# Leaving out GpSimd's normalisation of the attention weights: V as the streamed operand, with a column of ones

## The chip, the cores and the metric

The kernel runs on one core of a Trainium2 chip. The metric is the time of one execution on the device, in microseconds, as the median of several runs. The engines of a core work through queues of their own: TensorE (PE, with its weight loads as PEld), VectorE (DVE), ScalarE (ACT), GpSimd (POOL), and the sync engine (SP), which here issues nearly all transfers.

## The reference, cut to what matters

Three layers follow each other. Everything is float32.

1. Attention over 4 batches, 8 heads, 576 positions, 64 columns a head, causal with a window of 128 and a linear position bias:

```
scores = where(mask, q @ k.T / sqrt(64) + bias, -1e9);  e = exp(scores - max(scores))
attn_out = (e / (sum(e) + 1e-9)) @ v
```

2. A soft mixture of 8 experts with 4 slots each over the 2304 x 512 result `x`: `logits = x @ phi`; softmax over the tokens of a slot gives the slot inputs `d.T @ x`; each expert computes `relu(s @ w1[e]) @ w2[e]` (w1 and w2 together are 33.5 MB); softmax over the slots of a token combines the slot outputs.

3. A feed-forward layer: `h = x @ w_in; out = max(0.01 h, h) @ w_out`.

## The kernel before, in words

**Attention by pairs.** Two heads make a pair; 16 pairs (index i) run through a software pipeline. In `XO` each step of a pair has a place in units of one head; step `S` of pair i stands at 2 i + XO[S]. In `YO` the steps of a batch (8 heads) stand likewise. The program sorts all steps by place and emits them in this order, so that each engine's queue is in this order too, and several pairs are under way at once.

The steps of a pair: q and k are loaded, copied by GpSimd into another order of columns (`RK`, `RQ`, line L254), transposed by TensorE (`TK`, `TQ`, `TR`) and evacuated (`EK`, `EQ`, `ER`). `SX` and `SY` compute the scores in tiles of 64 x 192. VectorE adds the mask, writes the negated result and keeps the maximum (`M..`, L313). ScalarE takes the exponential and the row sum as accumulator (`E..`, L324). VectorE adds 1e-9 and inverts the sums (`UX`, `UY`, L330 and L331). GpSimd multiplies the weights by the inverses (`N..`, L338): nine instructions a pair. TensorE transposes the weights, 13 a pair (`F..`, L349), ScalarE and VectorE evacuate them (`C..`, L355).

`AV` (`attend`, L381) multiplies: V is the loaded operand and the transposed weights are streamed, 64 columns at a time, in 34 products. The result comes out with the head's columns on the partitions, as `xT`, which the logits need; it is evacuated by two ScalarE copies (L389) and a VectorE copy (L394), and a GpSimd copy (L397) pads the last 64 positions. `TX` transposes it back in five transposes (L404, L405), and VectorE copies the result into `xs` (`XS`, L409 and L410), which the slot inputs need.

**Scores' and outputs' buffers** in PSUM come from a ring of eight banks (`gt`), used in program order.

**Transfers.** Loads of q, k, v and the two shifts of v inside SBUF stand in the list `bulk`, with the place from which each may go; expert weights stand in the list `low`, in pieces of 128 x 512 (256 KB). `issue(n)` is called three times in each head unit, at the places of `XI`. It sends what is due of `bulk`; a call that sent nothing of it adds a credit (L0/3 pieces, after unit 26 L1/3) and sends as many pieces of `low` as the credit allows. A last call sends all that is left. 71 pieces have places that are free from the start (14 slots of four, and 15 others); six more go where q and k lay, and 20 where attention's other buffers lay, after the last pair's steps. The other 31 go into the slots p0 to p7 when the products with w1 have used them.

**The end of attention.** `TAIL` is the order of steps after the last `AV`. Then L776 multiplies the slot inputs by w1 (16 units of eight instructions) and L828 the hidden values by w2 (16 units). The first weights of the feed-forward layer, and then its products (L952), follow.

Of the kernel before, what the change touches and what calls it, by code (L numbers as in the profile page):

```python
# [18 lines left out]
def attn_softmoe_ffn(ctx: ExitStack, tc: tile.TileContext, q, k, v, phi, w1, w2, w_in, w_out, cst_in, out):  # L19
# [24 lines left out]
    YO = {"lg": 3.759, "lga": 4.885, "lh": 7.61, "lgc": 7.945, "lx": 8.496, "pm": 8.866, "ln": 9.053, "lnc": 9.191,  # L44
          "bm": 9.764, "tm2": 10.535, "tm3": 10.743, "bmv": 10.891, "dxv": 11.042, "bmx": 11.191, "tme": 11.431,
          "dxa": 11.452, "bt": 11.466, "btv": 12.289, "sl": 12.592, "bta": 12.637, "cb": 12.647, "slv": 12.811,
          "ds": 13.568, "cb2": 13.895, "cb3": 14.066, "dsv": 14.57, "cb4": 14.676}
    LAST = {"li": 6.795, "lgi": 6.853}
    ZA = {"DQK": 0.8, "DV": 0.3, "DVS": 0.3, "DVO": 1.4, "W0": -2.2, "EARLY": 0.8, "L0": 2.55, "L1": 3.6, "I1": 0.7769, "I2": 0.7995, "I3": 0.86}
# [1036 lines left out]
```

## Time and profile before

| | |
|---|---|
| median of 3 runs | 469.11 us (467.61 to 469.34) |
| profiled execution | 469.3 us, span 467.6 us, mean granted TensorE clock 0.967 of full |
| TensorE busy (loads) | 424.2 us, 91% (320.1 us, 68%) |
| VectorE, ScalarE, GpSimd busy | 245.7 us, 234.6 us, 144.2 us |
| transfers | 73.85 MB, 158 GB/s over the span |

The span runs from the first to the last instruction of the profiled execution; its own time is 1.7 us longer. A line number names the line of the kernel that issued an instruction. The granted clock is given as a share of 2.4 GHz.

### The profile page before, as it was taken

The page shows a single profiled execution, that of the slowest core. Times are in us where ns is not written, and L with a number is a line of the kernel's source. Part 1 is how long each engine was busy: PE and PEld are TensorE (multiplying, and loading weights), DVE is VectorE, ACT ScalarE, POOL GpSimd, SP SyncE. Part 2 cuts the span into 40 slices and gives each one's busy share as a digit, 9 for nine tenths or more (in the row PEclk, how much of TensorE's full clock was granted, in tenths as well). Part 3 has the DMA queues.
Part 4 walks back from the last instruction along what each step waited for, and adds up shares of the span by engine and source line. Part 5 has one row for each costly group of instructions (what it writes and reads, how often), then busy time and mean ns, then how long its engine had stood idle before and what let it go on. Part 6 is the DMA issues. An engine that isn't in the chain of part 4 may idle for free.

```text
span 467.6 us, 10684 instructions
## 1 busy us (share of the span) xinstructions
PE 424.2 (91%) x4012; PEld 320.1 (68%) x4012; DVE 245.7 (53%) x786; ACT 234.6 (50%) x706; POOL 144.2 (31%) x231
## 2 busy tenths in 40 slices
...
GB/s 156 149 219 208 148 227 171 178 187 173 177 178 193 117 239 379 382 382 386 392 405 391 208 78 2 179 1 0 1 1 1 1 0 137 0 0 136 0 69 68
DMA packets 63140, 73.85 MB, mean 158 GB/s; under 512 B 27760, under 2 KB 37360, under 8 KB 63088
## 3 DMA queue, kind: packets, MB, share of 16 engines
...
## 4 chain that ended last, share of the span: by engine, by line
PE 56%; POOL 5%; DMA 3%; SPq 2%; DVE 1%; issue 1%; ACT 0%; DVEq 0%; POOLq 0%
PE acc L952 42%; POOL ss L338 5%; PE ph L929 4%; PE pb L776 4%; DMA p<-in_moe_w_dram 3%; SPq L793 2%; PE ph L879 1%; DVE ss L313 1%; PE g L296 1%; PE ph L888 0%; PE pb L828 0%; PE g L622 0%; PE g L349 0%; PE g L381 0%; PE g L552 0%
## 5 line engine op out<-in xcount | busy, mean ns | idle before, releaser
L952 PE MATMUL acc<-p,p 128*128 128x512 f32 x648 | 158.9, 390 | 0.0
L952 PEld LDWEIGHTS acc<-p,p 128*128 128x128 f32 x648 | 120.7, 188 | 24.7 <-issue 1.7
L338 POOL TENSOR_SCALAR ss<-ss,sm 128x192 f32<-128x192 f32 (+1 forms) x144 | 102.3, 730 | 8.2 <-ACT ss L324 5.2
L942 DVE TENSOR_TENSOR p<-ar,p 128x384 fp32r<-128x384 f32 x96 | 53.1, 556 | 91.8 <-ACT ar L938 91.7
L934 ACT ACTIVATE p<-ph 128x384 fp32r<-128x384 f32 (+1 forms) x97 | 47.5, 491 | 92.7 <-PE ph L929 92.6
L349 PE MATMUL g<-ident,ss 128*128 128x128 f32 x208 | 45.3, 301 | 28.6 <-POOL ss L338 26.5
L324 ACT ACTIVATE ss<-ss,mx 128x192 f32<-128x192 f32 x144 | 61.8, 434 | 3.1 <-DVE mx L313 3.1
L349 PEld LDWEIGHTS g<-ident,ss 128*128 128x128 f32 x208 | 23.5, 142 | 45.9 <-POOL ss L338 44.6
L952 PE MATMUL acc<-b,p 128*128 128x512 f32 x216 | 53.9, 394 | 0.0
L722 POOL TENSOR_TENSOR p<-ar,p 128x512 fp32r<-128x512 f32 x8 | 10.6, 1324 | 136.0 <-ACT p L722 119.5
L938 ACT ACTIVATE ar<-ph 128x384 f32<-128x384 f32 x96 | 47.0, 490 | 0.0
L313 DVE CUSTOM_DVE_ANT_0 ss<-g,ar 128x192 f32<-128x192 f32 x128 | 38.6, 354 | 15.3 <-PE g L296 15.2
L952 PEld LDWEIGHTS acc<-b,p 128*128 128x128 f32 x216 | 40.1, 188 | 8.6 <-DVE ql L967 0.3
L355 ACT COPY pt<-g 128x384 f32<-128x384 f32 (+1 forms) x32 | 17.1, 533 | 49.8 <-PE g L349 49.8
L929 PE MATMUL ph<-p,p 128*128 128x384 f32 x96 | 33.1, 349 | 0.0
L254 POOL COPY ar<-ar 128x512 f32<-128x512 f32 x32 | 19.6, 615 | 40.6 <-issue 22.4
L381 PE MATMUL g<-pt,ar 64*64 64x64 f32 (+1 forms) x1088 | 30.2, 224 | 0.0
L381 PEld LDWEIGHTS g<-pt,ar 64*64 64x64 f32 (+1 forms) x1088 | 26.9, 136 | 3.7 <-DVE mx L313 1.0
L296 PE MATMUL g<-kqt 64*64 64x192 f32 (+2 forms) x768 | 29.1, 283 | 0.0
L296 PEld LDWEIGHTS g<-kqt 64*64 64x64 f32 x768 | 23.9, 135 | 5.9 <-issue 4.2
L324 ACT ACTIVATION_READ_ACCUMULATOR ss<-ss,mx 128x1 f32 x144 | 27.5, 191 | 0.0
L355 DVE COPY pt<-g 128x384 f32<-128x384 f32 x32 | 17.5, 548 | 17.0 <-PE g L349 17.0
...
## 6 DMA issues: line engine op xcount, KB each, us to landing
p<-in_moe_w_dram SPq DMA_DIRECT2D x56, 256.0 KB, 4.5
...
p<-in_moe_w_in_dram SPq DMA_DIRECT2D x5, 1024.0 KB, 10.7
...
out_dram<-ar SPq DMA_DIRECT2D x17, 256.0 KB, 2.1
ar<-in_q_dram SPq DMA_DIRECT2D x16, 256.0 KB, 3.4
...
ar<-in_moe_w_dram SPq DMA_DIRECT2D x16, 256.0 KB, 5.4
```

The costliest lines, as they stand in the source:

```text
L296: nc.tensor.matmul(sts[i, a, c][64 * u:64 * u + 64, o:o + n], lhsT=Q[r, 64 * e:64 * e + 64], rhs=K[r, 64 * e - 64 + k:64 * e - 64 + k + n] ...
L313: nc.vector.tensor_tensor_reduce(out=e[:, w], in0=p[:, w], in1=maskt[:, m:m + 192], op0=ALU.add, op1=ALU.min, accum_out=mx[i % 2][:, n:n + ...
L324: nc.scalar.activation(out=e[:, w], in_=e[:, w], func=AF.Exp, scale=-1.0, bias=mx[i % 2][:, n:n + 1], accum_out=sm[i % 2][:, n:n + 1])
L338: nc.gpsimd.tensor_scalar(out=e, in0=e, scalar1=sm[i % 2][:, n:n + 1], scalar2=None, op0=ALU.mult)
L349: nc.tensor.transpose(p[:, 128 * j:128 * j + 128], x, ident)
L355: (nc.vector.tensor_copy if a == 0 else nc.scalar.copy)(ptl[2 * a + c][:, 0:n], pts.pop((i, a, c))[:, 0:n])
L381: nc.tensor.matmul(o[t % 2][64 * a:64 * a + 64, x:x + 64], lhsT=V, rhs=P, start=t < 2 and u == 0 and j < 16, stop=t == 4 or (t == 3 and u ...
L929: nc.tensor.matmul(p, lhsT=mst[:, 128 * f:128 * f + 128], rhs=rhs, start=True, stop=True)
L934: nc.scalar.activation(out=G[t0, f][0][:, c], in_=H1[t0, f][:, c], func=AF.Prelu, alpha=0.01)
L938: nc.scalar.activation(out=gg, in_=H1.pop((t0, f)), func=AF.Prelu, alpha=0.01)
L942: nc.vector.tensor_tensor(out=g2, in0=G0.pop((t0, f)), in1=g1.bitcast(F32), op=ALU.subtract)
L952: nc.tensor.matmul(acc[t0][t], lhsT=(g1, g1, g2)[k][:, 128 * t:128 * t + 128], rhs=(WO1, WO2, WO1)[k][c][:, i], start=(f == f0 and k == 0) ...
```

## The change

ScalarE's exponentials no longer give row sums, and GpSimd no longer multiplies. V gets a 65th column that holds ones, and in `attend` the weights are the loaded operand and V is streamed, 65 columns at a time: the 65th column of a result is the sum of that row's weights. The result has positions on the partitions. `sums` adds 1e-9 to the sums and inverts them, `norm` multiplies the result by them, straight from PSUM into `xs`, both on VectorE. `TX` now transposes `xs`, ScalarE (`XT`) and VectorE (`XR`) copy that into `xT`. The tail begins with TX, XT, XR before the logits `lh`.

`issue` adds credit and sends pieces of `low` at every call, also at one that sent loads of `bulk`; L0 is 2.85 for 2.55; calls begin three units earlier, with no credit there. All places in `XO` and `YO` are new. Not shown: a few lines that follow from the names, and the conditions by which buffers are given to the weights after attention.

```diff
+    XO = {"RK": -5.833, "RQ": -4.884, "TR": -4.438, "TK": -4.435, "EK": -4.019, "ER": -3.744, "TQ": -3.472, "EQ": -3.389,
+          "SX": -2.632, "SY": -2.534, "MX0": -2.486, "MX1": -2.311, "MY1": -2.246, "MY0": -2.141, "EX0": -2.097,
+          "EX1": -1.867, "EY1": -1.854, "EY0": -1.635, "FY1": -1.428, "FX0": -1.417, "FX1": -1.356, "FY0": -1.277,
+          "CY1": -1.228, "CX0": -1.22, "CY0": -1.212, "CX1": -1.104, "AV": 0.067, "NS": 0.38, "NO": 0.724, "TX": 0.882,
+          "XR": 1.172, "XT": 1.455}
+    YO = {"lg": 4.307, "lga": 4.375, "lh": 8.258, "lgc": 8.43, "lx": 8.469, "pm": 9.118, "ln": 9.618, "bm": 9.798,
+          "bmv": 10.183, "bmx": 10.399, "lnc": 10.502, "bt": 10.836, "btv": 10.874, "dxv": 10.922, "tm2": 11.205,
+          "dxa": 11.366, "sl": 11.714, "bta": 11.761, "slv": 11.994, "tm3": 12.06, "tme": 12.179, "cb": 12.909,
+          "cb2": 12.964, "cb3": 13.232, "ds": 13.281, "dsv": 13.416, "cb4": 14.733}
+    ZA = {"DQK": 0.8, "DV": 0.3, "DVS": 0.3, "DVO": 1.4, "W0": -2.2, "EARLY": 0.8, "L0": 2.85, "L1": 3.6, "I1": 0.7769, "I2": 0.7995, "I3": 0.86}
-    VE, VW = 4 * VH * D, 9 * VH * D
+    VE, VU = 4 * VH * (D + 1), 9 * VH * (D + 1)
+    VW = -(-VU // 16) * 16
...
         def issue(n, low_max=0):
-            k = len(bulk)
             while bulk and bulk[0][2] <= n:
                 send()
-            if k == len(bulk):
-                credit[0] = min(credit[0], 1) + low_max
-                while credit[0] >= 1 and low and low[0][0] <= n:
-                    r, o, i = low.pop(0)
-                    nc.sync.dma_start(out=o, in_=i)
-                    credit[0] -= 1
+            credit[0] = min(credit[0], 1) + low_max
+            while credit[0] >= 1 and low and low[0][0] <= n:
+                r, o, i = low.pop(0)
+                nc.sync.dma_start(out=o, in_=i)
+                credit[0] -= 1
...
-                put(ve[i % NVB][:, :, a, :], v[b, h + a, 0:512, :].rearrange("(t p) d -> p t d", p=128), n + DVS * a, ("v", i))
-            put(vo[i % NVB][64:128, 4, :, :], v[b, h:h + VH, 512:S, :].rearrange("h p d -> p h d"), n + DVS, ("v", i))
+                put(ve[i % NVB][:, :, a, 0:D], v[b, h + a, 0:512, :].rearrange("(t p) d -> p t d", p=128), n + DVS * a, ("v", i))
+            put(vo[i % NVB][64:128, 4, :, 0:D], v[b, h:h + VH, 512:S, :].rearrange("h p d -> p h d"), n + DVS, ("v", i))
+            nc.vector.memset(ve[i][:, :, :, D:D + 1], 1.0)
+            nc.vector.memset(vo[i][64:128, 4, :, D:D + 1], 1.0)
+        for x in xs:
+            nc.vector.memset(x[64:128, 4], 0.0)
-                    nc.scalar.activation(out=e[:, w], in_=e[:, w], func=AF.Exp, scale=-1.0, bias=mx[i % 2][:, n:n + 1], accum_out=sm[i % 2][:, n:n + 1])
-            return f
-
-        def inv(c):
-            def f(i):
-                r = sm[i % 2][:, 4 * c:4 + 5 * c]
-                nc.vector.tensor_scalar(out=r, in0=r, scalar1=1e-9, scalar2=None, op0=ALU.add)
-                nc.vector.reciprocal(r, r)
-            return f
-
-        def norm(a, c):
-            def f(i):
-                jobs = [(ssl[2 * a + c][:, 192 * tt:192 * tt + 192], 4 * c + 2 * a + tt) for tt in range(2)] + [(ssl[0][:, RC:RC + 64], 8)] * (a == c == 1)
-                for e, n in jobs:
-                    nc.gpsimd.tensor_scalar(out=e, in0=e, scalar1=sm[i % 2][:, n:n + 1], scalar2=None, op0=ALU.mult)
+                    nc.scalar.activation(out=e[:, w], in_=e[:, w], func=AF.Exp, scale=-1.0, bias=mx[i % 2][:, n:n + 1])
             return f
 
...
-            os_[i] = o = [gt((128, 320)), gt((128, 256))]
+            W = D + 1
+            os_[i] = o = [gt((128, 6 * W)), gt((128, 4 * W))]
             jobs = []
             for t in range(4):
-                for u in range(2):
-                    for a in range(2):
-                        jobs.append((t, u, a, (E if u else O)[:, t, a, :], ptl[2 * a + t // 2][:, 128 * (t % 2) + 64 * u:128 * (t % 2) + 64 * u + 64]))
+                for a in range(2):
+                    for u in range(2):
+                        P = ptl[2 * a + t // 2][:, 128 * (t % 2) + 64 * u:128 * (t % 2) + 64 * u + 64]
+                        jobs.append((t % 2, u, t // 2 * 2 + a, 0, P, (E if u else O)[:, t, a, :], t < 2 and a == 0, False))
             for c in range(2):
-                for u in range(2):
-                    for a in range(2):
+                for a in range(2):
+                    for u in range(2):
                         for tt in range(2):
-                            t, r = 2 * c + tt, slice(64 * tt, 64 * tt + 64)
-                            e = 2 * t + 1 + u
+                            r, e = slice(64 * tt, 64 * tt + 64), 2 * (2 * c + tt) + 1 + u
                             V = E[r, e // 2, a, :] if e % 2 == tt else O[r, (e + 1) // 2, a, :]
-                            jobs.append((t, u, a, V, ptl[2 * a + c][r, 256 + 64 * u:320 + 64 * u]))
+                            jobs.append((tt, u, 2 * c + a, 64 * tt, ptl[2 * a + c][r, 256 + 64 * u:320 + 64 * u], V, False, c == a == 1 and (u or tt)))
             for a in range(2):
-                jobs.append((4, 0, a, E[0:64, 0, a, :], ptl[3][0:64, 384 + 64 * a:448 + 64 * a]))
-            for j, (t, u, a, V, P) in enumerate(jobs):
-                x = 128 * (t // 2) + 64 * u + 64 * (t % 2 == 0) if t < 4 else 0
-                nc.tensor.matmul(o[t % 2][64 * a:64 * a + 64, x:x + 64], lhsT=V, rhs=P, start=t < 2 and u == 0 and j < 16, stop=t == 4 or (t == 3 and u == 1 and j >= 16),
-                                 tile_position=((0 if j < 16 or t % 2 == 0 else 64), 64 * a))
+                jobs.append((0, 0, 4 + a, 0, ptl[3][0:64, 384 + 64 * a:448 + 64 * a], E[0:64, 0, a, :], False, a == 1))
+            for n, u, x, r, P, V, st, sp in jobs:
+                nc.tensor.matmul(o[n][64 * u:64 * u + 64, W * x:W * x + W], lhsT=P, rhs=V, start=bool(st), stop=bool(sp), tile_position=(r, 64 * u))
-        def evac_x(n):
-            def f(i):
-                p = os_[i][n][:, 64 * (1 - n):64 * (1 - n) + 256].rearrange("p (j c) -> p j c", j=2)
-                nc.scalar.copy(out=xT[:, i % 2, n:4:2, 0:128], in_=p)
-            return f
-
-        def evac_xr(i):
-            p = os_.pop(i)[0][:, 0:64]
-            nc.vector.tensor_copy(xT[:, i % 2, :, 128:144], p.rearrange("p (j c) -> p j c", j=4))
-
-        def pad_xr(i):
-            nc.gpsimd.tensor_copy(xTR[:, 0:64].rearrange("p (j c) -> p j c", j=4), xT[:, i % 2, :, 128:144])
+        rss = {}
+
+        def sums(i):
+            rss[i] = r = small.tile([128, 10], F32, tag="rs", name="rs", bufs=2)
+            o = [p.rearrange("p (x d) -> p x d", d=D + 1)[:, :, D] for p in os_[i]]
+            for c, x in ((slice(0, 4), o[0][:, 0:4]), (slice(4, 8), o[1])):
+                nc.vector.tensor_scalar(out=r[:, c], in0=x, scalar1=1e-9, scalar2=None, op0=ALU.add)
+            nc.vector.tensor_scalar(out=r[0:64, 8:10], in0=o[0][0:64, 4:6], scalar1=1e-9, scalar2=None, op0=ALU.add)
+            nc.vector.reciprocal(r[:, 0:8], r[:, 0:8])
+            nc.vector.reciprocal(r[0:64, 8:10], r[0:64, 8:10])
+
+        def norm(i):
+            r, os = rss.pop(i), os_.pop(i)
+            x = xs[(i // 2) % 3][:, :, 128 * (i % 2):128 * (i % 2) + 128].rearrange("p t (a d) -> p t a d", a=2)
+            for n in range(2):
+                o = os[n][:, 0:4 * (D + 1)].rearrange("p (t a d) -> p t a d", t=2, a=2)
+                nc.vector.tensor_tensor(out=x[:, n:4:2], in0=o[:, :, :, 0:D], in1=r[:, 4 * n:4 * n + 4].rearrange("p (t a) -> p t a", t=2).unsqueeze(3).to_broadcast([128, 2, 2, D]), op=ALU.mult)
+            o = os[0][0:64, 4 * (D + 1):].rearrange("p (a d) -> p a d", a=2)
+            nc.vector.tensor_tensor(out=x[0:64, 4], in0=o[:, :, 0:D], in1=r[0:64, 8:10].unsqueeze(2).to_broadcast([64, 2, D]), op=ALU.mult)
 
         xps = {}
 
         def turn_x(i):
             xps[i] = p = [gt(), gt((128, 128))]
+            x = xs[(i // 2) % 3][:, :, 128 * (i % 2):128 * (i % 2) + 128]
             for j in range(4):
-                nc.tensor.transpose(p[0][:, 128 * j:128 * j + 128], xT[:, i % 2, j, 0:128], ident)
-            nc.tensor.transpose(p[1], xTR, ident)
-
-        def evac_xs(i):
-            p, c = xps.pop(i), slice(128 * (i % 2), 128 * (i % 2) + 128)
-            nc.vector.tensor_copy(xs[(i // 2) % 3][:, 0:4, c], p[0].rearrange("p (t c) -> p t c", t=4))
-            nc.vector.tensor_copy(xs[(i // 2) % 3][:, 4, c], p[1])
+                nc.tensor.transpose(p[0][:, 128 * j:128 * j + 128], x[:, j], ident)
+            nc.tensor.transpose(p[1], x[:, 4], ident)
+
+        def evac_x(i):
+            nc.scalar.copy(out=xT[:, i % 2, :, 0:128], in_=xps[i][0].rearrange("p (j c) -> p j c", j=4))
+
+        def evac_xr(i):
+            nc.vector.tensor_copy(xT[:, i % 2, :, 128:144], xps[i][1][:, 0:64].rearrange("p (j c) -> p j c", j=4))
...
-        TAIL = ["lh", "TX", "lgc", "XS", "pm", "lx", "bm", "ln", "bmv", "dxv", "dxa", "bmx", "bt", "sl",
+                UNITS.update({f"M{n}{a}": smax(a, c), f"E{n}{a}": expo(a, c), f"F{n}{a}": flip(a, c), f"C{n}{a}": flip_c(a, c)})
+        TAIL = ["TX", "XT", "XR", "lh", "lgc", "pm", "lx", "bm", "ln", "bmv", "dxv", "dxa", "bmx", "bt", "sl",
                 "btv", "bta", "lnc", "slv", "ds", "dsv", "tm2", "tm3"]
-        for n in range(-3, NG + 3):
+        for n in range(-6, NG + 3):
             for x in XI:
-                ev.append((n + x, len(ev), lambda n=n, x=x: issue(n + x, (1 if n < 0 else L0 / 3 if n < 26 else L1 / 3))))
+                ev.append((n + x, len(ev), lambda n=n, x=x: issue(n + x, (0 if n < -3 else 1 if n < 0 else L0 / 3 if n < 26 else L1 / 3))))
         for _, _, f in sorted(ev, key=lambda e: e[:2]):
             f()
         issue(NG + 3, 40)
...
```

## Rows read from the trace of the kernel before

**Rows 1.** Instructions of TensorE in order of time: start, duration (us), line, operation, count.
```profile
21.64 0.47 PE L349 MATMUL g<-ident,ss 128*128 128x128 f32 x1 [6.96 <-POOL ss L338]
...
30.72 1.89 PE L381 MATMUL g<-pt,ar 128*64 128x64 f32 x68
...
39.86 1.89 PE L381 MATMUL g<-pt,ar 128*64 128x64 f32 x68
...
179.21 1.89 PE L381 MATMUL g<-pt,ar 128*64 128x64 f32 x68
```

**Rows 2.** Stretches: length, busy us of PE, PEld, DVE, ACT, POOL; clock, DMA share, GB/s.
```profile
39.86:179.21 139.35, 119.27 (x2205) 91.21 (x2204) 91.88 (x424) 90.80 (x355) 106.92 (x168) 1.00 0.68 188
...
39.86:167.00 127.14, 109.73 (x2045) 84.67 (x2045) 85.29 (x393) 84.41 (x330) 98.74 (x156) 1.00 0.65 177
...
191.63:209.33 17.70, 17.70 (x135) 5.21 (x138) 2.40 (x15) 1.28 (x4) 0.00 (x0) 0.84 1.04 385
...
222.39:235.07 12.68, 7.67 (x33) 0.84 (x32) 3.17 (x6) 1.20 (x2) 0.00 (x0) 0.59 1.05 391
235.07:241.44 6.37, 6.27 (x52) 5.37 (x48) 2.97 (x7) 3.65 (x11) 0.00 (x0) 0.75 1.04 404
241.44:467.60 226.16, 221.58 (x1006) 180.97 (x1004) 123.36 (x228) 116.79 (x259) 10.59 (x8) 1.00 0.20 73
```

**Rows 3.** Waits from 39.86 to 179.21: engine, line, releaser; total us, times, longest.
```profile
PE g L349 <- POOL ss L338: 17.9, 51, 0.4
```

**Rows 4.** GpSimd's groups by line, 39.86 to 179.21: busy us, mean ns, idle before.
```profile
L338 POOL TENSOR_SCALAR ss<-ss,sm 128x192 f32<-128x192 f32 (+1 forms) x126 | 89.5, 730 | 7.8 <-ACT ss L324 5.2 <-DVE col L576 1.1 <-DVE col L578 1.1
L254 POOL COPY ar<-ar 128x512 f32<-128x512 f32 x24 | 14.8, 616 | 22.4 <-issue 22.4
```

**Rows 5.** Transfers issued from 39.86 to 167: count, KB each, median us to landing.
```profile
DMA packets 31692, 22.47 MB, mean 177 GB/s; under 512 B 20071, under 2 KB 26535, under 8 KB 31666
...
p<-in_moe_w_dram SPq DMA_DIRECT2D x34, 256.0 KB, 4.1
...
ar<-in_k_dram SPq DMA_DIRECT2D x11, 256.0 KB, 3.0
```

**Rows 6.** The same view from 0 to 39.86, the expert weights.
```profile
p<-in_moe_w_dram SPq DMA_DIRECT2D x11, 256.0 KB, 4.8
```

**Rows 7.** TensorE in order of time behind attention: products with w1 and w2.
```profile
197.43 7.07 PE L776 MATMUL pb<-p,ar 128*32 128x512 f32 x64
...
225.19 1.93 PE L828 MATMUL pb<-p,ar 128*32 128x512 f32 x8 [2.79 <-DMA p<-in_moe_w_dram]
...
233.21 1.94 PE L828 MATMUL pb<-p,ar 128*32 128x512 f32 x8 [0.77 <-DMA p<-in_moe_w_dram]
```

**Rows 8.** ScalarE's groups by line, 39.86 to 179.21: the accumulator reads.
```profile
L324 ACT ACTIVATION_READ_ACCUMULATOR ss<-ss,mx 128x1 f32 x121 | 23.1, 191 | 0.0
```

**Rows 9.** VectorE's groups by line and shape, whole span.
```profile
L942 DVE TENSOR_TENSOR p<-ar,p 128x384 fp32r<-128x384 f32 x96 | 53.1, 556 | 91.8 <-ACT ar L938 91.7
L409 DVE COPY ar<-g 128x512 f32<-128x512 f32 x16 | 11.1, 692 | 11.7 <-PE g L404 11.7
...
L330 DVE TENSOR_SCALAR sm<-sm 128x4 f32<-128x4 f32 x16 | 4.3, 270 | 0.0
...
L331 DVE RECIPROCAL sm<-sm 128x4 f32<-128x4 f32 x16 | 2.8, 178 | 0.6
...
L450 DVE TENSOR_TENSOR ar<-ar,g 128x144 f32<-128x144 f32 x4 | 1.2, 301 | 0.1
```

**Rows 10.** Issues of lines L156 and L173, 39.86 to 167: ns min/median/max, first, last.
```profile
L156 SPq DMA_DIRECT2D ar<-in_v_dram x39: 378/541/1492, 41.8 to 164.1; - x39
...
L156 SPq DMA_DIRECT2D ar<-in_k_dram x22: 382/650/1358, 42.2 to 142.9; - x22
...
L173 SPq DMA_DIRECT2D p<-in_moe_w_dram x34: 430/590/1437, 39.8 to 165.5; - x34
```

**Rows 11.** GpSimd in order of time at the start.
```profile
20.22 0.62 POOL L254 COPY ar<-ar 128x512 f32<-128x512 f32 x1 [10.57 <-DMA ar<-in_k_dram]
```

More of the change, by code (lines that the diff above doesn't have):

```diff
@@ L37, in attn_softmoe_ffn @@
     WN = [5, 2, 0, 2, 3, 0, 0]
-    XO = {"RK": -5.642, "RQ": -4.656, "TK": -4.141, "TR": -3.873, "ER": -3.788, "EK": -3.357, "TQ": -3.304, "EQ": -3.071,
[5 rows of a table removed]
[L44 to L49, printed above, removed]
+    XO = {"RK": -5.833, "RQ": -4.884, "TR": -4.438, "TK": -4.435, "EK": -4.019, "ER": -3.744, "TQ": -3.472, "EQ": -3.389,
[4 rows of a table added]
+    YO = {"lg": 4.307, "lga": 4.375, "lh": 8.258, "lgc": 8.43, "lx": 8.469, "pm": 9.118, "ln": 9.618, "bm": 9.798,
+          "bmv": 10.183, "bmx": 10.399, "lnc": 10.502, "bt": 10.836, "btv": 10.874, "dxv": 10.922, "tm2": 11.205,
+          "dxa": 11.366, "sl": 11.714, "bta": 11.761, "slv": 11.994, "tm3": 12.06, "tme": 12.179, "cb": 12.909,
+          "cb2": 12.964, "cb3": 13.232, "ds": 13.281, "dsv": 13.416, "cb4": 14.733}
+    LAST = {"li": 6.35, "lgi": 6.568}
+    ZA = {"DQK": 0.8, "DV": 0.3, "DVS": 0.3, "DVO": 1.4, "W0": -2.2, "EARLY": 0.8, "L0": 2.85, "L1": 3.6, "I1": 0.7769, "I2": 0.7995, "I3": 0.86}
     DQK, DV, DVS, DVO, W0, EARLY = [ZA[x] for x in ("DQK", "DV", "DVS", "DVO", "W0", "EARLY")]
@@ L129, in attn_softmoe_ffn @@
         frx = fr.tile([128, 512], F32, name="frx")
-        xTR = fr.tile([128, 136], F32, name="xtr")[:, 0:128]
+        fr.tile([128, 136], F32, name="fpad")
         frp = [kqt[:, 512 * i:512 * i + 512] for i in range(5)] + ssl + ptl
         ve = [view(f"vt{i}", VE).rearrange("p (t h d) -> p t h d", t=4, h=VH) for i in range(NVB)]
-        vo = [view(f"vt{i}", VW - VE, VE).rearrange("p (t h d) -> p t h d", t=5, h=VH) for i in range(NVB)]
-        mx, sm = [[at.tile([128, 9], F32, name=f"{n}{i}") for i in range(2)] for n in ("mx", "sm")]
+        vo = [view(f"vt{i}", VU - VE, VE).rearrange("p (t h d) -> p t h d", t=5, h=VH) for i in range(NVB)]
+        mx = [at.tile([128, 9], F32, name=f"mx{i}") for i in range(2)]
         qsc = at.tile([128, 2 * HB], F32, name="qsc")
@@ L584, in attn_softmoe_ffn @@
         UNITS = {"TK": turn(0), "TQ": turn(1), "TR": turn_rest, "EK": evac_k, "EQ": evac_q, "ER": evac_rest, "SX": scores(0), "SY": scores(1),
-                 "RK": relay(0), "RQ": relay(1), "UX": inv(0), "UY": inv(1), "AV": attend, "XA": evac_x(0), "XB": evac_x(1), "XR": evac_xr, "XP": pad_xr, "TX": turn_x, "XS": evac_xs}
+                 "RK": relay(0), "RQ": relay(1), "AV": attend,
+                 "NS": sums, "NO": norm, "TX": turn_x, "XT": evac_x, "XR": evac_xr}
         for a in range(2):
             for c, n in enumerate("XY"):
-                UNITS.update({f"M{n}{a}": smax(a, c), f"E{n}{a}": expo(a, c), f"N{n}{a}": norm(a, c), f"F{n}{a}": flip(a, c), f"C{n}{a}": flip_c(a, c)})
-        TAIL = ["lh", "TX", "lgc", "XS", "pm", "lx", "bm", "ln", "bmv", "dxv", "dxa", "bmx", "bt", "sl",
+                UNITS.update({f"M{n}{a}": smax(a, c), f"E{n}{a}": expo(a, c), f"F{n}{a}": flip(a, c), f"C{n}{a}": flip_c(a, c)})
+        TAIL = ["TX", "XT", "XR", "lh", "lgc", "pm", "lx", "bm", "ln", "bmv", "dxv", "dxa", "bmx", "bt", "sl",
                 "btv", "bta", "lnc", "slv", "ds", "dsv", "tm2", "tm3"]
@@ L594, in attn_softmoe_ffn @@
         after = {}
-        YT = NG - 2 + max(XO[nm] for nm in ("XA", "XB", "XR", "XP"))
+        YT = NG - 2 + XO["NO"]
         ev = []
@@ L598, in attn_softmoe_ffn @@
             for i in range(NI):
-                y = YT + 1e-3 * (1 + TAIL.index((B - 1, nm))) if i == NI - 1 and nm in ("TX", "XS") else 2 * i + XO[nm]
+                y = YT + 1e-3 * (1 + TAIL.index((B - 1, nm))) if i == NI - 1 and nm in ("TX", "XT", "XR") else 2 * i + XO[nm]
                 ev.append((y, len(ev), lambda f=f, i=i: f(i)))
@@ L624, in to_siT @@
                 nc.scalar.copy(out=siT[:, g, c:c + 2, 16 * g:16 * g + 16], in_=p[:, :, 16 * g:16 * g + 16])
-        ev.append((NG - 2 + XO["MY1"] + .01, len(ev), lambda: nc.gpsimd.memset(siT, 0.0)))
+        ev.append((NG - 2 + max(XO[f"M{c}{a}"] for c in "XY" for a in range(2)) + .01, len(ev), lambda: nc.gpsimd.memset(siT, 0.0)))
         y = YT + 1e-3 * (1 + TAIL.index((B - 1, "ds")))
```

5 lines of the change are left out of this document (2 added, 3 removed), and 5 rows, old and new, of the table XO.

## The prediction

> **What bounds the kernel now.** I read TensorE in order of time first, then the table of stretches, the waits and groups by line of attention, the transfers, and the sync queue.
>
> Attention runs until the last of its 16 weighted sums (L381, `attend`, one for each pair of heads) starts at 179.21 us; the first starts at 30.72, the second at 39.86 [rows 1]. From the second to the last are 139.35 us for 14 pairs, 9.95 us a pair. In that stretch TensorE is busy 119.27 us, 8.52 a pair, VectorE 6.56, ScalarE 6.49, GpSimd 7.64 [rows 2]: no engine is full. TensorE's transposes of the weights (L349) wait 51 times, 17.9 us in all, for GpSimd's normalisation (L338) [rows 3], on which GpSimd spends 126 x 0.730 us, nine a pair, 6.4 of its 7.6 us [rows 4]. Attention is a loop through GpSimd.
>
> Then comes a stretch bounded by transfers: 385 GB/s, at a DMA share of 1.04 [rows 2]. It pays a debt. There is room for 71 pieces of expert weights (256 KB each) before attention gives up its own buffers; 34 were sent from 39.86 to 167 [rows 5] and 10 earlier (11 by the row, one of them at the border, in both) [rows 6]; 27 are owed. At the end TensorE waits for the last megabytes: four units of L828 start at 225.19 to 233.21, 2.67 us apart, each after a DMA wait [rows 7].
>
> From 241.44 the feed-forward part has TensorE busy 221.58 of 226.16 us at full clock [rows 2]; the change does not touch it.
>
> **The change part by part.** The sum is made against the profiled execution, 469.3 us (span 467.6 and 1.7 around it); the median of the runs is 469.11, 0.2 less, so the result stands for both.
>
> *GpSimd.* Nine multiplications and a small copy go; two copies L254 of 0.616 us stay [rows 4]. At 1.2 us a pair it can no longer be the bound.
>
> *ScalarE.* Nine accumulator reads of 0.191 us go [rows 8], overlapped by about half, so 0.9 us or more; two copies become one of the same columns. 6.5 falls to some 5.6.
>
> *VectorE.* Out: L330 and L331 twice, 2 x (0.27 + 0.18) = 0.9, and L409 with its neighbour of 128 columns, 0.69 + 0.29. In: `sums`, three additions and two reciprocals as small as those, 3 x 0.27 + 2 x 0.18 = 1.2; `norm`, three TENSOR_TENSOR of 256, 256 and 128 columns that no row shows. L450 (144 columns) takes 0.301, L942 (384) 0.556 [rows 9]: on their line 0.42, 0.42 and 0.28, together 1.1 (0.9 and 1.7 if each were its lower or its upper neighbour). The net is +0.4: 7.0 a pair.
>
> *TensorE.* The same products with operands exchanged, 65 columns streamed for 64: 1.89 x 1/64 = 0.03 us a pair. Five transposes stay five. Nothing is saved but waiting; part of the 8.52 is the exposed latency of transposes that came singly, so its work is some 8.0.
>
> *Transfers.* Each head unit (half a pair) gets 2.85 pieces, whether attention's own loads were sent at that tick or not: 5.7 a pair, where the rows show 34 in 12.8 pairs, 2.7. A piece of 0.262 MB costs 0.262/0.385 x 1.04 = 0.71 of share-time. From 39.86 to 167 the share-time is 0.65 x 127.14 = 82.6 [rows 2]; less 34 x 0.71 it leaves 58.5 for q, k, v and the shifts, 4.8 a pair. New demand: (4.8 + 4.0)/1.04 = 8.5 us a pair. The sync queue needs 0.54 for each of v and the shifts, 0.65 for each of q and k, 5.3 a pair for attention's nine, and 5.7 x 0.59 = 3.4 for the weights: 8.7 [rows 10]. So three resources come to lie between 8.0 and 8.7 while the weights last, about ten pairs; I take 9.0. For the last four pairs, when the 71 are through, 8.5. Bounds for a pair: 8.3 (below the three by what their counts may be off) and 9.95. 10 x 9.0 + 4 x 8.5 = 124 for 139.35: **-15.3** us.
>
> *Start.* GpSimd's copy of k for the third pair waited 10.57 us until 20.22 for its DMA, the first multiplications stood behind it in its queue [rows 11], and TensorE stood 6.96 us until 21.64 [rows 1]. Now nothing stands between exponentials and flips. What is late next are the third pair's transposes, which stand before the first weighted sum: k landed at 20.2, q is sent right behind and should be there 2 us later. So the first sum comes at about 24, and the second, one pair and the fourth pair's loads on, at 31 instead of 39.86: **-8.9** (bounds -4, if weights hold up that k, and -10).
>
> *Tail.* After the last sum come now `sums` and `norm`, transposes, a copy, and only then the logits; the two copies L409 and its neighbour leave. I count +0.6. The w1 products from 191.63 to 209.33 and the first twelve units of L828 until 222.39 run without a DMA wait and stay. But 27 pieces (7.1 MB, 18 us at 385 GB/s) are no longer owed, so the last loads follow the slots as L776 frees them: the ninth slot comes free 23 us after the last sum, and behind the one load that waits for it four stand, 2.7 us each; they are down after 23 + 2.5 + 5 x 2.7 = 39 us, and TensorE asks for the first of the four after 42. The last four units then take what units take without waiting, 0.88 (64 instructions, eight units, in 7.07 us [rows 7]), 3.5 in place of 235.07 - 222.39 = 12.68: -9.2. Together **-8.6** (0 to -9.5).
>
> *Clock.* TensorE's granted clock was 0.59 in the stretch with the DMA waits and 0.75 in the 6.37 us behind it [rows 2], between the levels of 1.2 and 2.4 GHz. Without the waits before it that stretch runs at the upper one; 6.27 x 0.75 = 4.7 is its shortest. Part of it is other engines' latency: **-1.3** (0 to -1.6).
>
> Sum: -15.3 - 8.9 - 8.6 - 1.3 = -34.1; 469.3 - 34.1 = 435.2, said as 435.
>
> **The rivals.** (a) *Another loop takes GpSimd's place.* VectorE works in order with `norm` between maxima and copies, and TensorE's transposes wait for `norm`. If attention falls only to 9.6 us a pair, 14 x 9.6 = 134 instead of 124, the time is 445; if not at all, 450. For it: today's 9.95 stands 17% over the busiest engine's 8.52. Against: without L338 the flips wait for exponentials alone, which run while TensorE does other products.
>
> (b) *The tail keeps its end*: the steady rate doesn't do what it says, or the last loads bind anyway: 435 + 8.6 + 1.3 = 445. Against: 71 pieces at 2.85 a unit need 25 units of the 32.
>
> (c) *Weights in front of k.* Loads of k take 3.0 us to land [rows 5] and are sent 1.39 head units ahead of their relay (tick -3.22, `RK` at -1.83 two pairs on), 6.2 us at the new pace. Three more pieces in front cost 3 x 0.68 = 2.0: hidden. If the backlog is a whole pair's weights, 3.9, the cover is gone and 0.7 us a pair show, 442; twice that backlog costs 4.6 a pair until the pacing follows, some 450.
> The Trainium skill, page "DMA: Bandwidth & Descriptors", section "Issuing engines are not separate DMA queues", says that transfers of every issuing engine run on the same 16 DMA engines and interleave, which speaks for this case.
>
> (d) *Slower: rows of V that no longer fit.* V now lands in rows of 64 values at a pitch of 65. Of the 4.8 us the bytes (13.6 MB in 12.4 pairs) would take 2.9 at the full rate; of the 1.9 above it V's 256-byte rows carry most, so V costs some 2.3. Were a row written so twice as dear, ten pairs took (8.8 + 2.3)/1.04 = 10.7 us and the kernel 452; from 2.8 times on it is slower than before, at three times (12.9 us) 476. Against: a pitch changes no count of packets.
> The same page's section "How a descriptor splits into AXI transactions" gives one extra transaction to a read that starts off a 256-byte boundary; if writes did the same, that would be the case of twice, 452 by that page. No run here shows it.
>
> **How the numbers follow.** Forecast 0.50, with 427 to 441 of its own; (a) 0.19, 442 to 451; (b) 0.11, 440 to 449; (c) 0.09, 440 to 450; (d) 0.06, half of it near 452 and half above 469; better than all, below 426 with attention at its floor, 0.05. The range is 425 to 453. Half a per cent, 2.3 us, is about what a measurement of this kernel can tell from none. Faster 0.94, same 0.02, slower 0.04.
>
> **What would show it.** Right: no wait of L349 for GpSimd; weighted sums 9 us apart and the second near 31; five to six weight issues a pair and none owed when attention ends; no DMA wait in the last units of L828. Wrong: TensorE waiting for VectorE's `norm` in every pair, GpSimd's copies waiting for k, or L828 still ending on a DMA.

## The result, and the profile after

The changed kernel takes 446.75 us (445.18 to 448.91, four runs) against 468.87 us for the kernel before on the same chip: a ratio of 0.9535 (95% interval 0.9482 to 0.9589), 22.1 us less. The forecast was 435. Its profiled execution takes 445.32 us, with a span of 443.6 us, 24.0 less than before. One execution of experiment 4 (463.28 us) ran in a slower state of the chip and is left out there.

First TensorE in order of time after (start, duration, line, operation, count; in brackets the idle time ahead and its releaser). L368 is the weighted sum (L381 before), L772 and L824 the products with w1 and w2 (L776 and L828 before), L948 the feed-forward products.

```profile
22.47 2.00 PE L368 MATMUL g<-ar,pt 128*64 128x65 f32 x68
29.23 1.99 PE L368 MATMUL g<-ar,pt 128*64 128x65 f32 x68
...
59.97 3.49 PE L368 MATMUL g<-ar,pt 128*64 128x65 f32 x68 [2.83 <-DMA ar<-ar]
70.42 1.99 PE L368 MATMUL g<-ar,pt 128*64 128x65 f32 x68
82.60 3.18 PE L368 MATMUL g<-ar,pt 128*64 128x65 f32 x68 [3.23 <-DMA ar<-ar]
...
135.37 1.99 PE L368 MATMUL g<-ar,pt 128*64 128x65 f32 x68
...
170.00 1.99 PE L368 MATMUL g<-ar,pt 128*64 128x65 f32 x68 [3.25 <-DMA ar<-ar]
...
181.42 2.78 PE L772 MATMUL pb<-p,ar 128*32 128x512 f32 x24 [0.36 <-ACT ar L620]
...
206.23 6.61 PE L824 MATMUL pb<-p,ar 128*32 128x512 f32 x59
212.78 0.49 PE L744 MATMUL w<-ident 128*128 128x128 f32 x2
```

The second sum starts at 29.23, 10.6 us earlier than before [rows 1]. From it to the last are 140.77 us, 1.4 **more** than before: 10.05 us a pair. L824 ends without a DMA wait, where four units had one each [rows 7]. The stretches (columns as in [rows 2]), the first split at the twelfth sum:

```profile
29.23:170.00 140.77, 113.69 (x2204) 101.45 (x2204) 88.77 (x460) 81.03 (x223) 16.03 (x28) 0.92 0.84 239
171.93:212.78 40.85, 38.61 (x353) 15.09 (x351) 12.00 (x53) 6.40 (x19) 7.39 (x19) 1.00 1.03 375
212.78:217.85 5.07, 4.82 (x51) 4.18 (x48) 2.99 (x7) 3.63 (x11) 0.00 (x0) 1.00 1.03 403
217.85:443.60 225.75, 221.97 (x1006) 180.99 (x1004) 123.27 (x228) 116.67 (x259) 10.78 (x8) 1.00 0.20 74
...
29.23:135.37 106.14, 84.91 (x1617) 75.52 (x1617) 64.33 (x335) 59.13 (x164) 12.97 (x22) 0.90 0.87 247
135.37:170.00 34.63, 28.78 (x588) 25.93 (x588) 24.44 (x128) 21.90 (x61) 3.06 (x6) 0.95 0.76 213
```

The account: start -10.6; attention +1.4; from the last sum's end to the end of the products with w2 40.79 for 53.97, -13.2 (before: 179.21 + 1.89 = 181.10 to 235.07; after: 170.00 + 1.99 = 171.99 to 212.78); the last sum itself +0.1; the clock stretch 5.07 for 6.37, -1.3; feed-forward -0.4. Together -24.0, the difference of the spans.

Inside attention, the ten pairs that carry weights take 10.61 us each, the last four 8.66. TensorE is *less* busy than before, 113.69 for 119.27 us; GpSimd falls from 106.92 to 16.03. What holds attention up stands in the waits from 29.23 to 170 (us in total, times, longest), and in the loads from 29.23 to 157 (count, KB each, median us to landing):

```profile
POOL ar L255 <- DMA ar<-in_k_dram: 67.2, 8, 9.3
DVE rs L378 <- PE g L368: 36.2, 14, 5.5
ACT kqt L277 <- PE g L262: 25.3, 11, 6.0
PE g L368 <- DMA ar<-ar: 19.1, 8, 3.3
```

```profile
ar<-in_v_dram SPq DMA_DIRECT2D x26, 128.0 KB, 4.0
ar<-in_k_dram SPq DMA_DIRECT2D x11, 256.0 KB, 4.8
```

The 17.9 us for GpSimd [rows 3] are gone. In their place TensorE stands 19.1 us at the sum, of 27.1 in which it idles (140.77 - 113.69), for `ar<-ar`: the two shifts of v inside SBUF, which can be issued only when v has landed. k lands after 4.8 us instead of 3.0 [rows 5]. The sync queue of one pair, in order (start, duration, line, target, count):

```profile
81.83 1.13 SPq L156 DMA_DIRECT2D ar<-in_k_dram  x2
83.05 1.25 SPq L156 DMA_DIRECT2D ar<-in_q_dram  x2
84.39 1.75 SPq L156 DMA_DIRECT2D ar<-in_v_dram  x3
86.20 1.86 SPq L171 DMA_DIRECT2D p<-in_moe_w_dram  x3
88.83 1.15 SPq L156 DMA_DIRECT2D ar<-ar  x2
90.01 1.56 SPq L171 DMA_DIRECT2D p<-in_moe_w_dram  x3
91.67 1.14 SPq L156 DMA_DIRECT2D ar<-in_k_dram  x2
```

Nearly no gap is left. So the queue itself (its issues, and its wait for v ahead of the shifts) was the first suspect; the DMA engines, at a share of 0.87, the second.

### The profile page after: what moved, and what is told of

The parts are those of the page before. It is cut to its first block, busy times and chain, and to the rows that moved or that the text cites. A ratio compares the mean times of both kernels' runs of the same rounds, so it can differ in the third digit from the quotient of the medians.

```text
span 443.6 us, 10375 instructions
## 1 busy us (share of the span) xinstructions
PE 406.3 (92%) x4012; PEld 326.6 (74%) x4012; DVE 241.5 (54%) x824; ACT 221.8 (50%) x546; POOL 40.2 (9%) x71
## 2 busy tenths in 40 slices
DMA packets 63137, 73.88 MB, mean 167 GB/s; under 512 B 27760, under 2 KB 37360, under 8 KB 63088
## 4 chain that ended last, share of the span: by engine, by line
PE 75%; DMA 17%; SPq 2%; DVE 2%; issue 1%; POOL 0%; ACT 0%; ACTq 0%; DVEq 0%; POOLq 0%
PE acc L948 45%; DMA ar<-ar 8%; PE g L368 7%; DMA ar<-in_v_dram 6%; PE ph L925 4%; PE pb L772 3%; PE pb L824 3%; PE g L336 2%; PE g L262 2%; PE g L297 2%; DVE ss L314 1%; SPq L171 1%; DMA p<-in_moe_w_dram 1%; PE g L150 1%; SPq L156 1%
## 5 line engine op out<-in xcount | busy, mean ns | idle before, releaser
L948 PE MATMUL acc<-p,p 128*128 128x512 f32 x648 | 158.8, 390 | 0.0
L948 PEld LDWEIGHTS acc<-p,p 128*128 128x128 f32 x648 | 120.7, 188 | 24.6 <-issue 1.7
L368 PE MATMUL g<-ar,pt 64*64 64x65 f32 (+1 forms) x1088 | 40.1, 253 | 26.4 <-DMA ar<-ar 22.4
L368 PEld LDWEIGHTS g<-ar,pt 64*64 64x64 f32 (+1 forms) x1088 | 36.2, 162 | 30.9 <-issue 15.2
L325 ACT ACTIVATE ss<-ss,mx 128x192 f32<-128x192 f32 x144 | 51.5, 431 | 14.3 <-DVE mx L314 14.3
L948 PE MATMUL acc<-b,p 128*128 128x512 f32 x216 | 54.4, 395 | 0.0
L948 PEld LDWEIGHTS acc<-b,p 128*128 128x128 f32 x216 | 40.1, 188 | 8.8 <-issue 0.2
L314 DVE CUSTOM_DVE_ANT_0 ss<-g,ar 128x192 f32<-128x192 f32 x128 | 38.2, 354 | 11.4 <-PE g L303 6.4
L297 PE MATMUL g<-kqt 64*64 64x192 f32 (+2 forms) x768 | 27.5, 281 | 0.0
L378 DVE TENSOR_SCALAR rs<-g 128x4 f32<-128x4 f32 x32 | 3.7, 157 | 42.5 <-PE g L368 42.5
L277 ACT ACTIVATE kqt<-g,qsc 128x512 f32<-128x512 f32 x16 | 11.0, 688 | 29.9 <-PE g L262 29.7
L336 PE MATMUL g<-ident,ss 128*128 128x128 f32 x208 | 25.9, 275 | 0.0
L718 DVE SCALAR_TENSOR_TENSOR ar<-ar 128x512 int32<-128x512 int32 x40 | 25.6, 684 | 0.2
L718 POOL TENSOR_TENSOR p<-ar,p 128x512 fp32r<-128x512 f32 x8 | 10.8, 1348 | 125.6 <-ACT p L718 109.0
L262 PE MATMUL g<-ident,ar 128*128 128x128 f32 x128 | 21.9, 298 | 0.0
## 6 DMA issues: line engine op xcount, KB each, us to landing
p<-in_moe_w_dram SPq DMA_DIRECT2D x7, 1024.0 KB, 11.4
```

The lines of the kernel that those rows point to most:

```text
L262: nc.tensor.transpose(p[:, bass.ds(t, 128, step=4)], natx[half][:, 128 * t:128 * t + 128], ident)
L297: nc.tensor.matmul(sts[i, a, c][64 * u:64 * u + 64, o:o + n], lhsT=Q[r, 64 * e:64 * e + 64], rhs=K[r, 64 * e - 64 + k:64 * e - 64 + k + n] ...
L314: nc.vector.tensor_tensor_reduce(out=e[:, w], in0=p[:, w], in1=maskt[:, m:m + 192], op0=ALU.add, op1=ALU.min, accum_out=mx[i % 2][:, n:n + ...
L336: nc.tensor.transpose(p[:, 128 * j:128 * j + 128], x, ident)
L368: nc.tensor.matmul(o[n][64 * u:64 * u + 64, W * x:W * x + W], lhsT=P, rhs=V, start=bool(st), stop=bool(sp), tile_position=(r, 64 * u))
L718: l.append(lambda: f(*a, **kw))
```

## The experiments

All start from the changed kernel unless it says otherwise; ratios are to the kernel before on the same chip. "The ten pairs" are those from the second weighted sum to the twelfth. Code is cut to the lines that matter. "L" or "Q" is the theory of the queue, "B" that of the DMA engines, "P" that of the places of the steps.

**1. Half the weight issues.** Weights for the slots p0 to p7 go as 512 KB transfers that cost two credits.

```diff
-                credit[0] -= 1
+                credit[0] -= o.shape[1]
-            pieces += [(W0, t[:, 512 * j:512 * j + 512]) for j in range(4)]
+            pieces += [(W0, t[:, 1024 * j:1024 * j + 1024]) for j in range(2)]
...
```

> The changed kernel, but weights for the p slots go out in transfers of 512 KB, two pieces each, and a transfer costs two credits: the same bytes at the same pace, half the issues (2.85 fewer a pair). Theory Q (the sync queue, which issues 9 + 5.7 transfers a pair one after the other and waits in its order for v before the shifts, bounds attention at 10.05 us a pair): 2.85 x 0.45 = 1.3 us less a pair, 8.7 to 9.0, weighted sums 2 to 16 in 122 to 126 us, time 429 to 434. Rival B (bandwidth: the 16 DMA engines at share 0.84 with loads of k landing after 4.8 us instead of 3.0): bytes are the same, 10.0 us a pair, 445 to 448. Rival P (the places written out in XO are at fault): unchanged, 445 to 448.

Measured: 447.3 us, 0.9532 (0.9475 to 0.9589), the same as the change and none of theory Q's gain; sums from 31.62 to 169.70, 9.86 a pair. The queue now waited longer for v (28.8 us over 15 waits, for 16.1 over 13 after). The count of issues alone is not the bound; that the wait took over was still possible.

**2. The arithmetic alone.** The old rule of `issue` and the old L0.

```diff
+            k = len(bulk)
...
-            credit[0] = min(credit[0], 1) + low_max
+            if k == len(bulk):
+                credit[0] = min(credit[0], 1) + low_max
...
-    "L0": 2.85
+    "L0": 2.55
```

> The changed kernel with the rule of issue() and L0 as before the change: the arithmetic part of the change alone. Weights fall back to about 2.7 pieces a pair. Theories Q and B alike: attention falls to 8.4 to 9.0 us a pair, since both the queue (5.1 + 1.6 us) and the DMA engines (6.5 us) have room, while about 27 pieces are owed again at the end and the tail gives back 10 to 13 us: 436 to 442. Rival P: 10 us a pair as in the changed kernel and the tail longer: 455 to 460.

Measured: 447.51 us, 0.9537 (0.9485 to 0.959), above the 436 to 442 that both theories expected. Attention first, then the stretch behind it (columns as in [rows 2]):

```profile
28.99:155.25 126.26, 108.60 (x2204) 96.48 (x2204) 88.70 (x460) 80.80 (x223) 15.86 (x28) 0.96 0.75 213
...
157.38:215.54 58.16, 46.15 (x352) 15.16 (x351) 11.88 (x53) 6.35 (x19) 7.35 (x19) 0.84 1.03 375
```

Attention takes 9.02 us a pair, close to the 8.9 forecast for the whole change, with 34 pieces in the ten pairs in place of 57. So rival P falls: the places in `XO` are those of the change. Yet the ten pairs alone take 9.37 us each, at a DMA share of 0.76, and TensorE still waits 12.5 us for the shifts in the whole of attention. The tail takes 58.16 us, 17.4 more than after, and ends on DMA waits again: more was owed than expected (60 pieces were issued by the end of the last sum, 64 before the change, 86 after). The sum is nearly the same: what the steady rate takes out of the tail it costs in attention.

**3. The steady rate alone**, in the kernel before (the edit of `issue`, L0 2.85, the earlier calls).

> The kernel before with the steady rate alone (rule of issue(), L0 2.85, earlier calls); GpSimd still normalises. Theory Q: two loops near 10 us a pair, GpSimd's and the queue's, interfere: 10.1 to 10.6 a pair, 2 to 9 us more in attention, and the tail 10 to 13 us shorter: 458 to 464. Rival B: the same within a few us. A gain of the tail near 13 us at an attention of 9.95 would be 456.

Measured: 457.9 us, 0.9772 (0.9712 to 0.9832), 0.1 us below theory Q's range: faster, though not surely by 2%. Attention takes 142.41 us, with GpSimd's waits (19.4 us), and the tail is short. Attention:

```profile
38.31:180.72 142.41, 121.11 (x2204) 92.36 (x2204) 91.23 (x424) 90.59 (x355) 106.42 (x168) 0.99 0.82 237
```

The parts don't add up: 4.6% for the arithmetic, 2.3% for the rate, 4.7% for both. The ten pairs show why: with 56 pieces in them they take 10.34 us each here, at a DMA share of 0.87, and 10.61 with 57 pieces and the same share in the changed kernel. At the steady rate, leaving out GpSimd's work shortens these pairs by nothing. Of the 10.8 us between the two spans (454.4 and 443.6), 9.1 lie ahead of the second sum (38.31 and 29.23).

**4. The shifts on ScalarE's queue**, so that the sync queue never waits for v.

```diff
-            o, i, _, _ = bulk.pop(0)
-            nc.sync.dma_start(out=o, in_=i)
+            o, i, _, _, e = bulk.pop(0)
+            e.dma_start(out=o, in_=i)
...
```

(`e` is `nc.scalar` for the two shifts and `nc.sync` for all else.)

> The changed kernel with the two shifts of v inside SBUF issued by ScalarE's queue instead of the sync queue, at the same places. Theory Q: the sync queue loses two issues (1.1 us) and its wait for v (16.1 us in 13 pairs, 1.2 a pair), so 8.4 to 9.2 us a pair and 430 to 437, if ScalarE, which now waits for v in its own order, has the room (5.8 busy of 10). Rival B: shifts move no fewer bytes, 10 us a pair, 445 to 448. Rival P: the weighted sums wait for the same shifts at the same places, 443 to 448.

Measured: 456.09 us, 0.9709 (0.9649 to 0.9769): above every range that was expected, and slower than the change. ScalarE itself now stands in the wait for v, and TensorE's transposes 23.7 us for ScalarE. The shifts land after 5.5 and 6.1 us (3.7 and 3.6 in the changed kernel, both from 40 to 150). The Trainium skill, page "DMA: Bandwidth & Descriptors", section "Issuing engines are not separate DMA queues", says that another issuing engine leads to the same 16 DMA engines. The trace agrees in so far as the shifts landed no sooner by the other queue.

**5, 6, 7. The shifts one unit later** (DVO 2.4): alone, with the 512 KB transfers of 1, and with fewer weights (L0 2.2).

```diff
-    "DVO": 1.4
+    "DVO": 2.4
```

> The changed kernel with DVO 2.4 for 1.4: the shifts of v stand one head unit later in the sync queue, behind the next pair's loads of k, q and v, so that v has landed when they are reached. Theory L (the queue is a chain of latencies: k, q and v issued in 5 us, then some 4 us until v has landed, with only weights to fill them, then shifts; half the weight issues changed nothing because the queue waited longer instead): the wait goes, 16.1 us over 13 pairs at least, 8.5 to 9.0 us a pair, 428 to 436. Rival B (the DMA engines, share 0.85 to 0.87 in attention, set the pace): 9.7 to 10 us a pair, 441 to 447. Rival P (the shifts are at fault by their place, later is worse): 10.5 us a pair or more, over 452.

> DVO 2.4 and the 512 KB transfers together. Theory L: with the wait gone the queue's own issue time counts again, 5.2 + 1.5 us a pair instead of 5.2 + 2.6; the DMA engines' 8.5 us or TensorE's 8.0 are then the bound: 8.4 to 8.7 us a pair, 427 to 432, at most 4 us under the kernel with DVO 2.4 alone. Rival B: 9.7 to 10 us a pair, 441 to 447.

> DVO 2.4 and L0 2.2 instead of 2.85: fewer weights a pair (4.4 for 5.7), 71 pieces still through by the end of attention. Theory L: the queue needs 5.2 + 2.0 us a pair and the DMA engines (4.8 + 3.1)/1.04 = 7.6: 8.2 to 8.6 us a pair, 425 to 432. Rival B: the pace follows the bytes, 10.05 x 7.6/8.5 = 9.0 us a pair, 431 to 436, and clearly faster than DVO 2.4 alone.

Measured: 451.37 us, 0.9632 (0.9601 to 0.9662); 451.0, 0.9642 (0.9605 to 0.9679); 445.7, 0.951 (0.9474 to 0.9547). The wait for v is nearly gone, but the shifts now stand in the queue behind v of the next pair, which needs the buffer that the running sum reads: a chain of sum, v, shift, sum, with 27.0 us of waiting for the shifts in 5. Experiments 5 and 6 lie above the ranges of both theories and don't tell them apart, since this chain is new. Only fewer weights helped (7), and it too ended above both ranges.

**8. The shifts one unit sooner** (DVO 0.4): more waiting in the queue, the same bytes.

> The opposite of e5: DVO 0.4, the shifts directly behind their own loads of v in the queue. Theory L: nothing fills the wait any more; three weight issues (1.3 us) that stood in it come on top: 11.0 to 11.5 us a pair, 458 to 466. Rival B: the same bytes, 10 us a pair, 445 to 449. Rival P (the shifts land too late for the sums): sooner is better, below 444.

Measured: 467.84 us, 0.9998 (0.9967 to 1.0029): the pair as theory L said, the time 1.8 us above its range. Attention, and the queue's wait:

```profile
28.95:188.25 159.30, 120.37 (x2205) 106.52 (x2204) 89.22 (x455) 81.16 (x223) 15.77 (x28) 0.86 0.72 202
```

```profile
SPq L156 <- DMA ar<-in_v_dram: 41.3, 16, 3.8
```

11.4 us a pair at a DMA share of 0.72: here the queue that stands still is the bound, not the DMA engines. So a wait in it can cost the whole gain; whether it costs anything at DVO 1.4 is another question.

**9, 10. The shifts between q and v of the next pair** (DVO 1.997): v has then long landed, and hardly a buffer is waited for. 10 has L0 2.3 too.

> The changed kernel with DVO 1.997: in the sync queue the shifts of a pair stand behind the next pair's loads of k and q and in front of its loads of v. With DVO 2.4 they stood behind that v, which is issued only when the weighted sum of the pair between is done, so that sum, v, shifts and the landing of shifts became one chain (10.4 us). Theory L: now neither wait stands in front of the shifts; the queue's issue time is 5.2 + 2.6 to 3.3 us a pair, the DMA engines need 8.5: 8.5 to 9.2 us a pair, 429 to 439. Rival B (DMA engines at 0.87 set the pace whatever the order): 9.8 to 10.1 us a pair, 443 to 448.

> DVO 1.997 and L0 2.3 instead of 2.85, 4.6 pieces a pair. Theory L: DMA engines (4.8 + 3.3)/1.04 = 7.8 us a pair, queue 5.2 + 2.3: the pace comes to TensorE's own 8.0 to 8.6, 424 to 433, and the pieces are still through at unit 30. Rival B: pace by bytes, 10.05 x 7.8/8.5 = 9.2 a pair, 433 to 439, with the same gain over e9 as e7 had over e5 (6 us).

Measured: 452.0 us, 0.9638 (0.962 to 0.9657), and 443.57, 0.9466 (0.9414 to 0.9518). The first ten pairs of each:

```profile
30.50:139.88 109.38, 83.20 (x1617) 74.18 (x1617) 65.17 (x341) 59.99 (x166) 13.46 (x23) 0.91 0.93 258
```

```profile
30.54:141.16 110.62, 90.33 (x1764) 80.77 (x1764) 72.16 (x374) 66.91 (x186) 14.64 (x25) 0.92 0.89 242
```

(The second row holds eleven pairs; its first ten, to 132.10, take 10.16 each.) In 9 the queue issues almost back to back, with 1.7 us of that wait left, and a pair takes 10.9 us, no less than after. Its loads land later: k after 6.6 us (5.0 in the changed kernel, both from 40 to 150). In 10, with 49 pieces in ten pairs for 60, a pair is 0.8 us shorter. Both missed theory L, and both lie above B's ranges too (443 to 448 and 433 to 439); but 10 gained 8.4 us on 9 where B said 6. As the queue of 9 was full with issues, it could still be the bound.

**11, 12. No wait for v and half the issues**: 9 and 10 with the 512 KB transfers.

> The shifts stand behind the next pair's k and q and ahead of its v, as in e9, and the expert weights' half of a pair goes in transfers of 512 KB at two credits each, so that neither the wait for v nor half of the weights' issues is left on the sync queue. Theory Q (the queue's issues and its wait together set a pair): 2.9 issues a pair fewer at about 0.5 us, 10.1 - 1.4 = about 8.7 us a pair against e9's 10.2, 14 pairs by 1.4 = 20 us less than e9, of which the tail takes little: 430 to 437 us, sums 30.5 to about 153. Rival B (the DMA engines at a share of about 0.9 set a pair, whatever the count of issues): 9.8 us a pair or more, share still about 0.9, queue with idle stretches but landings as late as in e9 (k 6 us or more, the shifts late at the weighted sums), 446 to 453 us.

> As e11, and with fewer weights a pair (L0 2.3 for 2.85 as in e10). Theory Q: a pair falls to the 8.3 to 8.7 us that TensorE's own work and the wait for exponentials leave, 425 to 434 us. Rival B: the bytes a pair are those of e10, so its 9.6 us a pair and its time, 441 to 446 us.

Measured: 453.35 us, 0.966 (0.9615 to 0.9704), and 445.16, 0.9488 (0.9439 to 0.9537). The ten pairs of 11, and its loads (40 to 150 us):

```profile
33.36:143.31 109.95, 83.02 (x1614) 73.76 (x1614) 65.74 (x337) 60.65 (x169) 13.40 (x23) 0.92 0.89 242
```

```profile
p<-in_moe_w_dram SPq DMA_DIRECT2D x21, 512.0 KB, 6.1
ar<-in_v_dram SPq DMA_DIRECT2D x22, 128.0 KB, 4.8
ar<-in_k_dram SPq DMA_DIRECT2D x10, 256.0 KB, 8.1
```

Two pairs of its queue:

```profile
91.04 1.29 SPq L156 DMA_DIRECT2D ar<-ar  x2
93.22 4.58 SPq L156 DMA_DIRECT2D ar<-in_v_dram  x3
97.85 1.61 SPq L171 DMA_DIRECT2D p<-in_moe_w_dram  x3
99.56 1.57 SPq L156 DMA_DIRECT2D ar<-in_k_dram  x2
101.22 1.32 SPq L156 DMA_DIRECT2D ar<-in_q_dram  x2
102.59 1.24 SPq L156 DMA_DIRECT2D ar<-ar  x2
104.17 3.95 SPq L156 DMA_DIRECT2D ar<-in_v_dram  x2
```

In the ten pairs 24 transfers took the place of 48, 2.4 issues a pair fewer, and nothing was won: 11.0 us a pair, k after 8.1 us. The time that the issues gave back turned up at v, 4.58 us for its three issues instead of 1.75. The issues themselves got no longer (0.37, 0.37 and 0.65 us); the queue stood still between them, and its largest wait in attention (30 to 165 us), by the profile, is now for the weights' own transfers:

```profile
SPq L156 <- DMA p<-in_moe_w_dram: 17.5, 15, 3.1
...
SPq L156 <- DMA ar<-in_v_dram: 5.7, 2, 3.4
```

Theory Q expected 430 to 437 and 425 to 434 and falls. B expected 446 to 453 and 441 to 446: 11 lies 0.35 us above its range, 12 inside. Why the queue waits for those transfers, of which v needs nothing, stays open.

## Why the prediction was right and wrong

**Right: the direction, and the end of the loop through GpSimd.** The transposes no longer wait for another engine at all; their group over the whole span (busy us, mean ns, idle before):

```profile
L336 PE MATMUL g<-ident,ss 128*128 128x128 f32 x208 | 25.9, 275 | 0.0
```

*Start*: -8.9 forecast, -10.6 measured. *Clock*: -1.3 and -1.3. *Tail*: -8.6 and -13.2. The part of the w2 products went as worked out (-9.2 forecast, -9.3 measured). The chain up to the first w1 product got 1.1 us shorter where +0.6 was counted, and the w1 products took 14.93 us for 17.70; their stretch had been at a granted clock of 0.84 [rows 2], and the whole tail now runs at 1.00. Start and tail both passed the bounds that they were given (-10 and -9.5).

**Wrong: the ten pairs with weights at 9.0 us**, and so the forecast's own range of 427 to 441. They took 10.61. The last four, without p0 to p7 to fill, took 8.66 where 8.5 was said. The term was forecast at -15.3 and came out at +1.4, 16.8 us off; start, tail and the rest won 6.7 more than forecast (0.4 of it in the feed-forward part), which leaves the 10.1 by which the profiled execution lies above 435.2. So the time lies within 425 to 453 partly by luck: what the middle lost, start and tail gave back in part, beyond their own bounds, and the upper part of the range was there for the rivals.

The step that failed is "(4.8 + 4.0)/1.04 = 8.5", and "I take 9.0" from three resources near 8.5. Its numerator was nearly right: 0.87 x 106.14 = 92 us of share-time in ten pairs, 9.2 a pair for 8.8. At a share of 1.04 that would still be 8.9 a pair, so the divisor carries the rest of the miss. 1.04 is the share of the stretch in which weights alone stream [rows 2]; with attention's loads in the mix the ten pairs of no run had a mean above 0.93. The reading that fits, argued and not shown by itself: the loads, shifts and sums depend on each other, so as the engines fill up each landing comes later (k 3.0 us before, 4.8 after, 6.6 and 8.1 in experiments 9 and 11), and the pair grows before the mean share reaches 1. Part of the price is TensorE's clock: five of the ten weighted sums ran at a granted clock of 0.50 to 0.76 behind a wait, and together took 6.2 us longer than 1.99 each.

Three smaller slips changed little. VectorE was said to go up, to 7.0 us a pair, and went down, to 88.77/14 = 6.3. The 58.5 us of share-time over the 12.4 pairs that the prediction names under (d) are 4.7 a pair and not 4.8. Under (d) three times the cost of V's rows gives 474 by the prediction's own sum, and not 476.

What sets the ten pairs, as far as shown: the weights' bytes, not the count of issues and not the wait for v alone. By pieces in ten pairs (a 512 KB transfer counts as two): 34 pieces, 9.37 us a pair (experiment 2, to 122.69); 48, 10.11 (7); 49, 10.16 (10) and 10.58 (12, from 28.91 to 134.69); 57, 10.36 (1) and 10.61 (after); 60, 10.94 (9) and 11.00 (11); 61, 10.91 (5) and 11.00 (6). Only experiment 8, whose queue stands still, falls out, with 54 and 12.23. From 34 to 60 that is 1.6 us for 2.6 pieces, 0.6 a piece; in the tail a piece costs 0.262/0.385 = 0.68. So sending it early wins next to nothing, which is why the steady rate brought nothing on top of the arithmetic (2) though it brought 11 us by itself (3).

Not settled: how the 10.6 us divide into DMA engines that are full and landings that are merely late. In slices of 2 us the share of the changed kernel's ten pairs runs from 0.43 to 1.17, and 11 of 53 slices stand at 1.00 or more. So the mix does fill the engines at times, and 0.87 is a mean with slack in it, not a ceiling: latency has a part. Experiment 8 shows that the order of the queue can bind at 0.72, and experiment 2 that 9.0 is not reached in the ten pairs even with 34 pieces.

**The rivals.** (a) VectorE as the new loop: its time range held the result, its mechanism did not show; no wait of TensorE for `norm` is among the large ones, and experiment 2 with the same VectorE work ran at 9.02. (b) fell with the tail's -13.2. (c), weights in front of attention's loads, was right in kind, and its range (440 to 450) held the time too. Its place was not: k's wait (67.2 us of idle GpSimd) is not where TensorE stood, the shifts' was. The rule of the Trainium skill named there (page "DMA: Bandwidth & Descriptors", section "Issuing engines are not separate DMA queues"), that all transfers share the same 16 engines, agrees with experiment 4, and with 11, where k lands later beside larger weight transfers. (d) fell: in experiment 2, with the same rows of V, the share-time left for attention's loads is (0.75 x 103.09 - 37 x 0.71)/11 = 4.6 us a pair, where 4.8 was reckoned before the change, and the packets of the whole run stay the same (63137 for 63140). In the changed kernel the same sum gives 5.2, far from the 2.3 more that (d) asked for.
